# Block-sparse attention and a token/channel mixer in one kernel: keys of two head pairs turned by DMA, and the first pair's keys written from PSUM

## The chip, the cores and the metric

The kernel runs on one core of a Trainium2 chip. The metric is the device time of one execution in microseconds, the median of several runs. A profiled execution gives a trace of every instruction; its span is a little shorter than the time of that execution, which has some work around it. The engines are named as in the profile: PE multiplies matrices (PEld is its weight load), DVE and ACT are the vector and the scalar engine, POOL is GpSimd, SP issues most DMA transfers from one queue, in order.

## The reference

Inputs are `q`, `k`, `v` of shape (4, 8, 768, 64) and the weights of a mixer. Attention picks key blocks of 64 by the mean of their keys, then the mixer works on the result:

```python
k_rep = k.reshape(B, H, n_blocks, block, D).mean(axis=3)
gate_scores = np.einsum('bhsd,bhnd->bhsn', q, k_rep)      # 12 blocks
gate_scores = np.where(causal, gate_scores, -1e9)
# each query keeps its 3 best blocks and its own block, causally
scores = scale * np.matmul(q, k.transpose(0, 1, 3, 2))
attn = softmax(np.where(mask, scores, -1e9))
x = np.matmul(attn, v)                                    # heads side by side: (4, 768, 512)
h = np.maximum(x.transpose(0, 2, 1) @ w_tok1, 0) @ w_tok2 # along the tokens
u = x + h.transpose(0, 2, 1)
out = u + np.maximum(u @ w_ch1, 0) @ w_ch2                # along the channels
```

Which blocks a query keeps depends on close comparisons, so the gate's operands are carried in more than one fp16 number; the scores themselves take fp16.

## The kernel before, in words

**Tiling.** Heads go in 16 pairs, `i` = 0 to 15; four pairs make one batch element `b`. The two heads of a pair fill the 128 partitions (64 dimensions each) when the dimensions lie in partitions, and stand side by side when tokens lie in partitions. A sequence is six tiles of 128 tokens, twelve blocks of 64.

**Preparation of a pair's keys.** `load_qk` (line 350) loads them in fp32 with tokens in partitions (tile `kl`). PE turns them with six fp32 transposes into PSUM: `transposes` (line 406, into a two-bank buffer of the ring `big`, which the scores also use) or, for the pairs below `SPLIT` = 4, `transposes_half` (line 414, three at a time into one bank of the ring `bank`). ACT or DVE then evicts them, times eight, into an fp32 tile `kt` (`evac_t` and `evac_half`, through `scaled` at lines 434 and 436). POOL casts each head's 64 rows to fp16 into the matmul operand `KA` (`cast`, line 490). DVE sums the columns of each block (`ksum`, line 563; for pair 0 straight from PSUM, `ksum_half`, line 428). The sums become the gate's operand: for pairs 0 to 3 in fp32 (`kcopy`, line 516), from pair 4 on as an fp16 number and its fp16 rest (`split_k`, lines 508 and 510).

**Preparation of a pair's queries.** Pairs 0 to 3 go the same way as the keys (`qt`). Pairs 4 to 9 are evicted as an fp16 number and its rest (`evac_q` line 449, `rest_q` line 456). From pair 10 on (`QTURN`) the queries are rounded while tokens are still in partitions: ACT writes the fp16 number (`split_hi`, line 464), DVE the rest (`split_rest`, line 470), and two DMA transposes from SP turn both (`turn_q`, line 475). POOL places each head's rows in the operand `QA`, copying two fp16 numbers as one fp32 (`place_q`, line 496).

**Gate and mask.** PE multiplies queries by block sums (line 525 in fp32, line 541 in fp16 parts), DVE finds the third best (lines 531 to 601), and the resulting mask is turned, by PE (line 611) up to pair 8 and by DMA (line 590) from pair 9 on, and put in twelve further rows of `QA`: the mask rides in the scores' matmul (line 633). ACT takes the exponential (line 647), PE multiplies with the values (line 663), DVE normalises (lines 671 and 682).

**Mixer.** When the four pairs of a batch element are done, PE does the token mix (lines 706 and 718; for `b` = 0 per pair, lines 737 and 751), then the first channel product (line 787) and the second (line 838, in seven products per four blocks; line 894 at the very end).

**What sets the order.** Nothing is ordered by hand. Each step is an `Op` with an engine, a planned duration, its dependencies, the buffers that it takes and a priority. `plan` (line 102) runs through them once, before the kernel is built: on each engine it takes, of what can start soon, the op with the smallest priority, and for steps given with `either` also the engine, ACT or DVE, that ends sooner. The result is a fixed sequence per engine; every engine then works through its own in order. A pair's priorities are ten per pair plus an offset: `PRE[i]` for its preparation, `LAG[b]` for the channel products, `SHIFT` for steps of one kind. Ahead of 17 us of planned time PE's holes are filled with dummy matmuls (line 913). Weights are loaded by POOL (lines 942 to 947); `WAIT` names for each load the cast that it is placed behind, `W0` that of the first, the token weights. SP issues key, query and value loads, turns (`SPO`) and output stores in one sequence; the ring `kt` has three slots, `kl` three, `bank` three, `big` two.

Of the kernel before, what the change touches and what calls it, by code (L numbers as in the profile page):

```python
# [54 lines left out]
HEAD = 15000.0  # L55
INBANK = 16
QTURN = 10
MTURN = 9
TOCC = 1250
QLEAD = 0.0  # L60
# [188 lines left out]
def kernel(  # L249
# [28 lines left out]
    pairs = [(b, h) for b in range(B) for h in range(0, H, 2)]  # L278
    NP = len(pairs)
    RINGS = dict(big=2, bank=3, av=1, ql=3, kl=3, v32=2, kt=3, gs=2, e0=3, e1=3, e2=3, rc=2,  # L280
                 x16=2, h1=1, u=2, uT=1, h2a=1, h2b=1, ob=3, s1=1, s3=1, s4=1, f32=6, qh=2, qr=2, mt=1)

    def const(name, a, dt, eng):
        t = sp.tile(list(a.shape), dt, tag=name, name=name)
# [3 lines left out]
    def sb(tag, shape, dt, name):  # L288
        return sp.tile(shape, dt, tag=tag, bufs=RINGS[tag], name=name)
# [26 lines left out]
    t3_16 = sp.tile([128, HF, 256], F16, tag="t3", name="t3")  # L316
    t4_16 = sp.tile([128, HF, 256], F16, tag="t4", name="t4")
    warm = t1_16[:, 0, :]
    spare = sp.tile([128, 8], F16, tag="spare", name="spare")
    ident32 = sp.tile([128, 128], FP, tag="id32", name="id32")  # L320
    ident16 = sp.tile([128, 128], F16, tag="id16", name="id16")
# [13 lines left out]
    def act(cols, deps, prio, fn, takes=()):  # L335
        return op("ACT", 70 + cols * 0.833, 173 + cols * 0.833, deps, prio, fn, takes)
# [80 lines left out]
    def evac_half(name, src, i, m):  # L417
# [3 lines left out]
            scaled(e, T[name, i][:, S // 2 * m:S // 2 * m + S // 2], T["tr", src, i, m])  # L421
        return f

    def ksum_half(i, m):
        def f():
            if ("kst", i) not in T:
                T["kst", i] = sp.tile([128, NB], FP, tag="kst", bufs=2, name=f"kst_{i}")
            nc.vector.tensor_reduce(out=T["kst", i][:, NB // 2 * m:NB // 2 * m + NB // 2],
                                    in_=T["tr", "kl", i, m].rearrange("p (n w) -> p n w", w=64), axis=AX.X, op=ALU.add)
        return f  # L430
# [21 lines left out]
    def rest_q(i):  # L452
        def f():
            t = sb("qr", [128, S - 128], F16, f"qr_{i}")
            T["qr", i] = t
            nc.vector.scalar_tensor_tensor(out=t, in0=T["tr", "ql", i][:, 128:S], scalar=UP, in1=T["qh", i][:, 128:S],
                                           op0=ALU.mult, op1=ALU.subtract)
        return f

    def split_hi(i):  # L460
# [489 lines left out]
    for i in range(NP):  # L950
# [8 lines left out]
        zq = [op("POOL", 355, 412, [], pre - 1, zero_q(i))] if 0 < i < R else []  # L959
        for t32, src, off in (("kl", k, 0), ("ql", q, 0.1)):  # L960
            bf = Buf(t32)
            if t32 == "ql" and i >= QTURN:
# [16 lines left out]
                O[t32, i] = op("SP", 950, 0, [], pre - 12 + off, load_qk(i, t32, src), [bf], size=1900)  # L979
            name = "kt" if t32 == "kl" else "qt"  # L980
            if i < SPLIT:
                tb = Buf("kt")
                ev, ks = [], []
                for m in range(2):
                    bk = Buf("bank")
                    tr = pe(330, [O["ld", t32, i, m] if i < HALVES else O[t32, i]], pre + off + 0.01 * m, transposes_half(t32, i, m), [bk], tail=320)
                    bf.users.append(tr)
                    first = name == "kt" and i < EARLY
                    if first:
                        ks.append(dve(460, [tr], pre + 0.4, ksum_half(i, m)))  # L990
# [4 lines left out]
                O[name, i], O["half", name, i] = ev[1], ev  # L995
            else:
                big = Buf("big")
                O["tr", t32, i] = pe(660, [O[t32, i]], pre + off, transposes(t32, i), [big], tail=320)
                bf.users.append(O["tr", t32, i])
            if name == "kt":  # L1000
                if i >= SPLIT:
                    tb = Buf("kt")
                    O["kt", i] = either(768, 860, [O["tr", t32, i]], pre + 0.5, evac_t("kt", "kl", i), [tb])
                    big.users.append(O["kt", i])
                for x in range(2):
                    if i < HALVES:
                        for m in range(2):
# [12 lines left out]
                if i < HALVES:  # L1020
                    pass
                elif i < SPLIT:
                    O["kcopy", i] = dve(257, [O["ksum", i]], pre + 1, kcopy(i))
                else:
                    O["kcopy", i] = op("POOL", 1040, 998, [O["ksum", i], O.get(("gate", i - 2))], pre + 1, split_k(i))
            elif i < SPLIT:
                qb = tb
                for x in range(2):
                    if i < HALVES:
                        for m in range(2):  # L1030
                            O["cast", "qt", i, x, m] = op("POOL", 470, 500, ev[m:m + 1] + zq, pre + 4.1 + 0.2 * m, cast(QA, "qt", i, x, S // 2 * m, S // 2 * m + S // 2))
                            qb.users.append(O["cast", "qt", i, x, m])
                        continue
                    O["cast", "qt", i, x] = op("POOL", 865, 822, [O["qt", i]] + zq + last_scores(x), pre + 4.1, cast(QA, "qt", i, x))
                    qb.users.append(O["cast", "qt", i, x])
            else:
                hb, rb = Buf("qh"), Buf("qr")
                O["qh", i] = act(768, [O["tr", t32, i]], pre + 0.6, evac_q(i), [hb])
                O["qr", i] = dve(740, [O["qh", i]], pre + 2, rest_q(i), [rb])
                big.users.append(O["qr", i])  # L1040
                hb.users.append(O["qr", i])
                for x in range(2):
                    O["cast", "qt", i, x] = op("POOL", 457, 503, [O["qh", i]] + zq + last_scores(x), pre + 4.1, place_q(i, x))
                    hb.users.append(O["cast", "qt", i, x])
# [248 lines left out]
    with tc.manual_schedule():  # L1293
# [75 lines left out]
```

## Time and profile before

| | us |
|---|---|
| median of 3 runs | 250.09 (250.06 to 250.19) |
| the profiled execution | 250.11 |
| its span | 248.30 |
| PE busy | 238.0 |
| DVE busy | 185.4 |
| ACT busy | 155.3 |
| POOL busy | 136.2 |
| last transposes of keys (pair 15, line 406) | at 172.3 |
| last wait of the span: final add and store after the last matmul | 245.0 to 248.3 |

The page of the profile gives busy time per engine first. It counts instructions as they overlap: a matmul's record is longer than the time by which it holds up the next one, so what a group of matmuls costs is read from the starts, or from the chain of waits, which tells the pieces in order of time. In rows by engine, a bracket says how long the engine sat idle before the instruction and what ended that.

### The profile page before, as it was taken

The numbers are of one execution on the slowest core, as the hardware profiler recorded it, in microseconds if no ns is written. First come the engines' busy times: TensorE is split into PE (matmuls) and PEld (weight loads), VectorE is DVE, ScalarE is ACT, GpSimd is POOL, SyncE is SP. The second block draws the span as 40 slices with busy tenths as digits, with TensorE's granted clock in tenths as the row PEclk, the third lists the DMA queues.
The fourth block names the chain that finished last, engine by engine and source line by source line (L and its number), as shares of the span: only waits on it lengthen the run. The fifth ranks groups of instructions, "written<-read, shape, count | busy, mean of one in ns | idle before, by whom it ended". The sixth has DMA issues, their size and how long they took to land.

```text
span 248.3 us, 6734 instructions
## 1 busy us (share of the span) xinstructions
PE 238.0 (96%) x2575; PEld 181.8 (73%) x2575; DVE 185.4 (75%) x572; ACT 155.3 (63%) x234; POOL 136.2 (55%) x230
## 2 busy tenths in 40 slices
PE   7898989999999899999999989999999999999994
PEld 5787879767767676888666878677666867766863
DVE  6677768977999799998956999995654769332742
ACT  3576777998688878356656958756687631355210
POOL 8967826465643773589985799706410245500380
PEclk9999999999999999999999999999999999999999
DMA  8999999999992199989999946463210024600033
GB/s 163 204 210 230 194 234 222 192 201 237 181 222 36 29 233 206 189 175 207 240 213 223 205 87 102 105 122 76 87 26 3 1 76 97 195 19 0 3 124 131
DMA packets 105040, 35.38 MB, mean 143 GB/s; under 512 B 98672, under 2 KB 101512, under 8 KB 105008
## 3 DMA queue, kind: packets, MB, share of 16 engines
q1 hardware_dynamic: 100016, 30.45, 62.2%
q0 software_dynamic: 3392, 4.11, 9.9%
q10 hardware_dynamic: 1600, 0.39, 0.8%
q8 instruction: 20, 0.33, 0.6%
q14 instruction: 12, 0.10, 0.1%
HBM read 26.92 MB, written 6.29 MB: 134 GB/s over the span
## 4 chain that ended last, share of the span: by engine, by line
PE 81%; POOL 5%; issue 5%; ACT 3%; DVE 3%; DMA 2%; SPq 1%; POOLq 0%; DVEq 0%; ACTq 0%
PE c L787 23%; PE c L838 18%; PE sps L633 12%; PE aps L663 8%; PE ups L718 3%; PE tok L706 3%; PE tkl L406 3%; PE c L894 2%; PE gps L525 2%; DMA kl<-in_k_dram 2%; ACT e L647 2%; PE tok L737 1%; PE gps L541 1%; PE sps L637 1%; POOL kp L508 1%
## 5 line engine op out<-in xcount | busy, mean ns | idle before, releaser
L647 ACT ACTIVATE e<-sps 128x1024 f16<-128x1024 f32 (+2 forms) x96 | 85.1, 916 | 18.3 <-PE sps L633 15.2
L787 PE MATMUL c<-uT,wc 128*128 128x256 f16 (+1 forms) x384 | 69.3, 326 | 0.0
L633 PE MATMUL sps<-Q,KA 76*128 76x128 f16 (+7 forms) x384 | 52.0, 259 | 1.9 <-ACT e L647 1.1
L860 POOL TENSOR_TENSOR vu<-v,u 128x256 f32<-128x256 f32 x33 | 22.9, 719 | 51.7 <-DVE v L853 51.7
L787 PEld LDWEIGHTS <-wc 128*128 128x128 f16 x384 | 36.2, 98 | 19.6 <-issue 0.2
L490 POOL CAST KA<-kt 64x768 f16<-64x768 f32 (+1 forms) x34 | 27.8, 819 | 30.6 <-ACT kt L434 19.9
L633 PEld LDWEIGHTS <-KA 76*128 76x128 f16 (+1 forms) x384 | 31.3, 98 | 15.2 <-ACT e L647 1.6
L663 PEld LDWEIGHTS <-e 128*128 128x128 f16 x672 | 24.9, 98 | 3.3 <-issue 0.4
L663 PE MATMUL aps<-V,e 128*128 128x65 f16 x672 | 26.6, 193 | 0.4 <-POOL V L383 0.3
L689 ACT ACTIVATE h2a<-c 128x512 f16<-128x512 f32 (+1 forms) x29 | 15.2, 528 | 11.7 <-PE c L787 11.5
L689 ACT ACTIVATE h2b<-c 128x512 f16<-128x512 f32 (+1 forms) x31 | 15.9, 527 | 10.2 <-PE c L787 10.1
L838 PEld LDWEIGHTS <-s 128*128 128x128 f16 x198 | 18.8, 98 | 3.6 <-issue 1.1
L838 PE MATMUL c<-t,s 128*128 128x256 f16 x132 | 17.8, 272 | 1.0 <-DVE ob L874 1.0
L682 DVE TENSOR_TENSOR x<-aps,rc 128x384 f16<-128x384 f32 x32 | 17.6, 550 | 0.5
L653 DVE TENSOR_TENSOR e<-e,m 128x768 f16<-128x768 f16 x24 | 14.6, 608 | 3.6 <-ACT e L647 3.5
L691 DVE TENSOR_SCALAR h2a<-c 128x256 f16<-128x256 f32 (+1 forms) x19 | 9.0, 476 | 10.7 <-PE c L787 10.6
L434 ACT ACTIVATE kt<-tkl 128x768 f32<-128x768 f32 (+1 forms) x16 | 11.7, 729 | 6.6 <-PE tkl L406 3.3
L496 POOL COPY Q<-qh 64x384 f32<-64x384 f32 x24 | 13.8, 576 | 2.2 <-ACT qh L449 1.2
L383 POOL CAST V<-v 128x768 f16<-128x768 f32 x16 | 13.6, 856 | 2.4 <-DMA v<-in_v_dram 1.9
L572 DVE MAX8 m<-gps 128x8 f32<-128x12 f32 x160 | 13.9, 158 | 0.3
L563 DVE TENSOR_REDUCE kst<-kt 128x12 f32<-128x768 f32 x15 | 14.1, 943 | 0.0
L691 DVE TENSOR_SCALAR h2b<-c 128x256 f16<-128x256 f32 (+1 forms) x17 | 8.0, 468 | 8.3 <-PE c L787 8.0
(117 smaller groups left out, 434.1 us busy)
## 6 DMA issues: line engine op xcount, KB each, us to landing
v<-in_v_dram SPq DMA_DIRECT2D x16, 384.0 KB, 5.8
out_dram<-ob SPq DMA_DIRECT2D x23, 256.0 KB, 2.5
kl<-in_k_dram SPq DMA_DIRECT2D x30, 192.0 KB, 5.0
ql<-in_q_dram SPq DMA_DIRECT2D x30, 192.0 KB, 5.1
wc<-in_moe_w_ch_dram POOLq DMA_DIRECT2D x8, 384.0 KB, 6.7
w<-in_moe_w_tok_dram POOLq DMA_DIRECT2D x2, 384.0 KB, 6.5
ql<-in_q_dram ACTq DMA_DIRECT2D x4, 96.0 KB, 3.5
kl<-in_k_dram SPq DMA_DIRECT2D x4, 96.0 KB, 3.1
```

The costliest lines, as they stand in the source:

```text
L490: nc.gpsimd.tensor_copy(out=dst[i % R][x][lo:lo + 64, a:z], in_=T[name, i][lo:lo + 64, a:z])
L563: nc.vector.tensor_reduce(out=kst, in_=T["kt", i].rearrange("p (n w) -> p n w", w=64), axis=AX.X, op=ALU.add)
L633: nc.tensor.matmul(out=p[:, off + a:off + a + n], lhsT=KA[i % R][x][0:rows, 128 * kk:128 * kk + 128], rhs=QA[i % R][x][0:rows, q0 + a:q0 + ...
L647: nc.scalar.activation(out=e[:, 0:width], in_=T["sps", i, x, g][:, 0:width], func=AF.Exp, scale=scale)
L653: nc.vector.tensor_tensor(out=d, in0=d, in1=m0.broadcast_to([128, NJ, 128]), op=ALU.mult)
L663: nc.tensor.matmul(out=p[:, jq, :], lhsT=T["e", i, x, g][:, o:o + 128], rhs=V16[i % (R + 1)][:, x, kk, :], start=(kk == 0), stop=(kk == jq))
L682: nc.vector.tensor_tensor(out=T["x16", b][:, :, 64 * hh:64 * hh + 64], in0=T["aps", i, x][:, :, 0:64], in1=T["rc", i, x].broadcast_to([128 ...
L689: e.activation(out=out, in_=src, func=AF.Relu)
L691: e.tensor_scalar(out=out, in0=src, scalar1=0.0, scalar2=None, op0=ALU.max)
L787: nc.tensor.matmul(out=p, lhsT=wc1_16[:, cc, 128 * fc:128 * fc + 128], rhs=T["uT", b][:, a // 128:e // 128, cc, :], start=(cc == 0), stop= ...
L838: nc.tensor.matmul(out=T["c2" + key, b, j], lhsT=x[:, fc, :], rhs=y[:, fc, :], start=first and fc == 0, stop=fc == HF - 1, skip_group_chec ...
L860: nc.gpsimd.tensor_tensor(out=t, in0=T["v", b, j], in1=T["u", b][:, j + 3 * row, 256 * col:256 * col + 256], op=ALU.add)
```

## The change

It has three parts. **Pairs 14 and 15** (`KTURN`): the keys are rounded with tokens in partitions, the fp16 number by ACT or DVE (`ksplit_hi`) and its rest by DVE (`ksplit_rest`), into one slot of the ring `kt`; a DMA transpose from SP turns the fp16 numbers (`turn_k`) into a new tile `kh` with one slot; POOL places each head's rows as fp32 words (`place_k`). The block sums come from PE: for each of six token tiles and both parts a matmul with the 128x128 part as weight and a constant `two` of two columns (ones in the first 64 rows, ones in the last 64), so that twelve matmuls give twelve block sums in one bank (`ksum_pe`); ACT or DVE copies them out (`ksum_put`). The rounding of a pair's queries is made to wait for that of its keys. **Pair 0**: the fp32 tile `kt` and its four POOL casts go; instead each head's 64 rows of each half go from PSUM to `KA` as fp16, by ACT or DVE (`place_half`), after the block sums of that half. **The order**: `PRE`, `LAG`, `SHIFT` and `W0` have new values; among them pair 0's offset goes from 9.0 to 3.0, and the token weights are placed behind the second query cast of pair 2 in place of the first key cast of pair 3. The preamble fills `two` with three DVE instructions.

```diff
-PRE = [9.0, 1.5, 3.5, 1.5, 4.5, 4.0, 2.5, 3.0, -3.0, -0.5, 8.5, 9.5, 6.0, 8.5, -1.0, -2.5]
-LAG = [5.0, 1.0, -2.0, -2.0]
-SHIFT = {'bias': 0.5, 'sc': -0.7, 'ex': -3.2, 'uadd': 1.0, 'lt': 3.7, 'ch1': -0.8, 'qn2': -0.5, 'av': 1.2, 'tok1': -7.0, 'gate': -0.5, 'qr': 2.3, 'mask': 0.8, 'ksum': 0.5, 'cast': -2.0, 'dg': 2.8, 'half': -0.7, 'top': 3.2, 'put': -1.5, 'kt': -4.0, 'gm': 1.0, 'norm': 1.2, 'kcopy': -6.0, 'tr': 0.5, 'qn': -3.0}
+PRE = [3.0, 1.5, 0.5, 0.5, 3.5, 4.0, 5.0, 5.5, -3.5, -0.5, 9.5, 10.5, 3.0, 6.0, -3.5, -2.0]
+LAG = [5.0, 0.0, 9.0, 6.5]
+SHIFT = {'bias': 0.5, 'sc': -0.7, 'ex': -3.2, 'uadd': 1.0, 'lt': 4.2, 'ch1': -0.8, 'qn2': 2.5, 'av': 2.0, 'tok1': -8.0, 'gate': -0.5, 'qr': 1.2999999999999998, 'mask': -2.0, 'ksum': -0.5, 'cast': -1.5, 'dg': 2.5, 'half': -1.7, 'top': 0.2, 'put': -0.5, 'kt': -4.0, 'gm': -2.7, 'norm': 1.4, 'kcopy': 0.0, 'tr': 0.5, 'v': -1.0, 'relu2': 1.0, 'umix': -0.5, 'relu1': 1.0, 'qh': -4.0}
...
+KTURN = 14
+KHN = 1
...
-W0 = ('kt', 3, 0)
+W0 = ('qt', 2, 1)
...
+    def place_half(i, x, m):
+        def f(e):
+            rows, cols = slice(64 * x, 64 * x + 64), slice(S // 2 * m, S // 2 * m + S // 2)
+            scaled(e, KA[i % R][x][rows, cols], T["tr", "kl", i, m][rows, :])
+        return f
...
+            scaled(e, t[:, 0], T["kl", i])
...
+            nc.vector.scalar_tensor_tensor(out=t[:, 1], in0=T["kl", i], scalar=UP, in1=t[:, 0], op0=ALU.mult, op1=ALU.subtract)
...
+            turn(T["kh", i].rearrange("p (j t) -> p j t", t=128), T["kn", i][:, 0].rearrange("p j d -> p (j d)"))
...
+            nc.gpsimd.tensor_copy(out=KA[i % R][x][lo:lo + 64, :].bitcast(FP), in_=T["kh", i][lo:lo + 64, :].bitcast(FP))
...
+            for j in range(NJ):
+                for c in range(2):
+                    nc.tensor.matmul(out=p[:, 2 * j:2 * j + 2], lhsT=T["kn", i][:, c, j, :], rhs=two, start=(c == 0), stop=(c == 1))
...
+            if t32 == "kl" and i >= KTURN:
+                O[t32, i] = op("SP", 950, 0, [], pre - 12.1 - QLEAD, load_qk(i, t32, src), [bf], size=1900)
+                nb, hb, kb = Buf("kt"), Buf("kh"), Buf("bank")
+                O["kn", i] = either(768, 860, [O[t32, i], O.get(("qn", i - 1))], pre - 4.1, ksplit_hi(i), [nb])
+                O["kn2", i] = dve(940, [O["kn", i]], pre - 4.1, ksplit_rest(i), both=True)
...
+                O["kh", i] = op("SPO", TOCC, 0, [O["kn", i], O.get(("kh", i - 1))], -1.1, turn_k(i), [hb], size=1300)
+                O["ksm", i] = pe(420, [O["kn2", i]], pre + 0.2, ksum_pe(i), [kb])
...
+                O["ksum", i] = either(80, 140, [O["ksm", i]], pre + 0.5, ksum_put(i))
...
+                O["kcopy", i] = op("POOL", 1040, 998, [O["ksum", i], O.get(("gate", i - 2))], pre + 1, split_k(i))
+                for x in range(2):
+                    O["cast", "kt", i, x] = op("POOL", 457, 503, [O["kh", i]] + last_scores(x), pre + 4, place_k(i, x))
...
-                O["qn", i] = act(795, [O[t32, i]], pre - 4, split_hi(i), [nb])
+                O["qn", i] = act(795, [O[t32, i], O.get(("kn", i))], pre - 4, split_hi(i), [nb])
...
-                tb = Buf("kt")
+                tb = Buf("kt") if i >= HALVES or name == "qt" else None
...
+                    if i < HALVES and name == "kt":
+                        for x in range(2):
+                            O["cast", "kt", i, x, m] = either(384, 460, [tr] + ks[m:m + 1], pre + 0.6 + 0.3 * x, place_half(i, x, m))
+                            bk.users.append(O["cast", "kt", i, x, m])
+                        continue
...
-                        for m in range(2):
-                            O["cast", "kt", i, x, m] = op("POOL", 470, 500, ev[m:m + 1], pre + 4 + 0.2 * m, cast(KA, "kt", i, x, S // 2 * m, S // 2 * m + S // 2))
-                            tb.users.append(O["cast", "kt", i, x, m])
+                        continue
...
+        nc.vector.memset(two, 0.0)
+        for n in range(2):
+            nc.vector.memset(two[64 * n:64 * n + 64, n:n + 1], 1.0)
```

More of the change, by code (lines that the diff above doesn't have):

```diff
@@ L280 @@
     RINGS = dict(big=2, bank=3, av=1, ql=3, kl=3, v32=2, kt=3, gs=2, e0=3, e1=3, e2=3, rc=2,
-                 x16=2, h1=1, u=2, uT=1, h2a=1, h2b=1, ob=3, s1=1, s3=1, s4=1, f32=6, qh=2, qr=2, mt=1)
+                 x16=2, h1=1, u=2, uT=1, h2a=1, h2b=1, ob=3, s1=1, s3=1, s4=1, f32=6, qh=2, qr=2, mt=1, kh=KHN)
     def const(name, a, dt, eng):
@@ L318 @@
     warm = t1_16[:, 0, :]
+    two = sp.tile([128, 2], F16, tag="two", name="two")
     spare = sp.tile([128, 8], F16, tag="spare", name="spare")
@@ L457, in f, with ksplit_hi, ksplit_rest, turn_k @@
                                            op0=ALU.mult, op1=ALU.subtract)
+        return f
+    def ksplit_hi(i):
+        def f(e):
+            t = sb("kt", [128, S], FP, f"kn_{i}").bitcast(F16).rearrange("p (c j d) -> p c j d", c=2, d=2 * D)
+            T["kn", i] = t
+            scaled(e, t[:, 0], T["kl", i])
+        return f
+    def ksplit_rest(i):
+        def f():
+            t = T["kn", i]
+            nc.vector.scalar_tensor_tensor(out=t[:, 1], in0=T["kl", i], scalar=UP, in1=t[:, 0], op0=ALU.mult, op1=ALU.subtract)
+        return f
+    def turn_k(i):
+        def f():
+            T["kh", i] = sb("kh", [128, S], F16, f"kh_{i}")
+            turn(T["kh", i].rearrange("p (j t) -> p j t", t=128), T["kn", i][:, 0].rearrange("p j d -> p (j d)"))
+        return f
+    def place_k(i, x):
+        def f():
+            lo = 64 * x
+            nc.gpsimd.tensor_copy(out=KA[i % R][x][lo:lo + 64, :].bitcast(FP), in_=T["kh", i][lo:lo + 64, :].bitcast(FP))
+        return f
+    def ksum_pe(i):
+        def f():
+            p = ps("bank", [128, NB], "kps")
+            T["kps", i] = p
+            for j in range(NJ):
+                for c in range(2):
+                    nc.tensor.matmul(out=p[:, 2 * j:2 * j + 2], lhsT=T["kn", i][:, c, j, :], rhs=two, start=(c == 0), stop=(c == 1))
+        return f
+    def ksum_put(i):
+        def f(e):
+            kst = sp.tile([128, NB], FP, tag="kst", bufs=2, name=f"kst_{i}")
+            T["kst", i] = kst
+            copy(e, kst, T["kps", i])
         return f
@@ L961 @@
             bf = Buf(t32)
+            if t32 == "kl" and i >= KTURN:
[3 more added lines that the diff above has]
+                O["kn2", i] = dve(940, [O["kn", i]], pre - 4.1, ksplit_rest(i), both=True)
+                bf.users += [O["kn", i], O["kn2", i]]
+                O["kh", i] = op("SPO", TOCC, 0, [O["kn", i], O.get(("kh", i - 1))], -1.1, turn_k(i), [hb], size=1300)
+                O["ksm", i] = pe(420, [O["kn2", i]], pre + 0.2, ksum_pe(i), [kb])
+                nb.users += [O["kh", i], O["ksm", i]]
+                O["ksum", i] = either(80, 140, [O["ksm", i]], pre + 0.5, ksum_put(i))
+                kb.users.append(O["ksum", i])
+                O["kcopy", i] = op("POOL", 1040, 998, [O["ksum", i], O.get(("gate", i - 2))], pre + 1, split_k(i))
+                for x in range(2):
+                    O["cast", "kt", i, x] = op("POOL", 457, 503, [O["kh", i]] + last_scores(x), pre + 4, place_k(i, x))
+                    hb.users.append(O["cast", "kt", i, x])
+                continue
             if t32 == "ql" and i >= QTURN:
@@ L992 @@
                             O["kcopy", i, m] = dve(257, ks[m:], pre + 0.45, kcopy(i, NB // 2 * m, NB // 2 * m + NB // 2))
+                    if i < HALVES and name == "kt":
[3 more added lines that the diff above has]
+                        continue
                     ev.append(either(384, 460, [tr] + ks[m:m + 1] + (ev if i >= HALVES else []), pre + 0.5 + off, evac_half(name, t32, i, m), [tb] if m == 0 else []))
                     bk.users += ks[m:m + 1] + ev[m:m + 1]
-                O[name, i], O["half", name, i] = ev[1], ev
+                if ev:
+                    O[name, i], O["half", name, i] = ev[1], ev
             else:
@@ L1006 @@
                     if i < HALVES:
-                        for m in range(2):
-                            O["cast", "kt", i, x, m] = op("POOL", 470, 500, ev[m:m + 1], pre + 4 + 0.2 * m, cast(KA, "kt", i, x, S // 2 * m, S // 2 * m + S // 2))
-                            tb.users.append(O["cast", "kt", i, x, m])
+                        continue
                     else:
```

## The prediction

> **What bounds the kernel now.** I read the first page for the engines' shares, then busy time by stretches of 10 us, then the list of what the matmul engine (PE) waited for, and last the chain of waits with the timelines of the stretches that the change touches.
>
> ```profile
> span 248.3 us, 6734 instructions
> PE 238.0 (96%) x2575; PEld 181.8 (73%) x2575; DVE 185.4 (75%) x572; ACT 155.3 (63%) x234; POOL 136.2 (55%) x230
> ```
>
> PE is busy 238.0 of 248.3 us, so 10.3 us are idle. The average hides where. The stretches (columns: stretch, its length, then busy us and count for PE, PEld, DVE, ACT, POOL, then granted clock and DMA) show it:
>
> ```profile
> 10.00:20.00 10.00, 9.06 (x108) 7.94 (x108) 7.40 (x33) 7.96 (x13) 7.55 (x12) 1.00 1.21 214
> 140.00:150.00 10.00, 9.01 (x116) 7.70 (x115) 9.85 (x19) 6.49 (x9) 9.38 (x16) 1.00 0.67 140
> 170.00:180.00 10.00, 10.00 (x113) 7.02 (x110) 6.04 (x24) 6.17 (x11) 6.23 (x13) 1.00 0.23 70
> 240.00:248.30 8.30, 5.03 (x36) 3.23 (x33) 2.10 (x5) 0.00 (x0) 1.82 (x3) 1.00 0.34 127
> ```
>
> From 150 to 230 us PE is never idle, and the granted clock is 1.00. There a microsecond of PE work is a microsecond of the end. The last 3.3 us (8.30 less 5.03) are the final add and store, which the change leaves alone. All else that can be won lies before 60 us and in two single waits later. The list of PE's waits names them (total, times, longest):
>
> ```profile
> PE c L838 <- DVE ob L874: 1.0, 1, 1.0
> PE gps L541 <- POOL kp L510: 0.8, 1, 0.8
> PE sps L633 <- ACT Q L695: 0.6, 1, 0.6
> PE tok L737 <- DVE x L682: 0.5, 1, 0.5
> ```
>
> With these go two waits for exps (0.80 at 32.06, 0.30 at 27.81), one of 0.27 for values at 53.85 and one of 0.21 for block sums at 20.78: 4.5 us in all behind 15 us of the span. Ahead of that, PE fills its holes with dummy matmuls, 6.5 us of them, which are no work.
>
> **Part 1: keys of pairs 14 and 15.** Removed per pair: six fp32 transposes on PE, their eviction and the sum over 768 columns. Added: a rounding and a rest in token layout, one DMA turn, twelve fp16 matmuls of two columns, a small copy, two placings. What PE pays for the transposes is read from the chain; what a short fp16 matmul with a new 128x128 weight costs, from the gate matmuls of 48 columns, whose busy times overlap, so the starts count:
>
> ```profile
> 172.47 0.66 PE tkl L406 x6
> ```
>
> ```profile
> 151.98 0.19 PE L541 MATMUL gps<-kp,qh 128*128 128x48 f16 x1
> 152.01 0.18 PE L541 MATMUL gps<-kp,qr 128*128 128x48 f16 x1
> ...
> 152.21 0.18 PE L541 MATMUL gps<-kp,qr 128*128 128x48 f16 x1
> 152.24 0.83 PE L663 MATMUL aps<-V,e 128*128 128x65 f16 x21
> ```
>
> Ten of them take 152.24 - 151.98 = 0.26 us, 26 ns each. Two columns aren't in the trace. Above, they are bounded by the fp32 gate matmuls (line 525, ten in 1.11 us, 0.11 each: 1.33 us per pair, a loss of 0.67); below, they can't be free, since each loads a weight of its own, and I put the floor at half the 48-column row, 0.16 us. I take 26 ns, the row with the same type and the same weight load: 12 x 0.026 = 0.31 us. **PE saves 2 x (0.66 - 0.31) = 0.70 us**, between a gain of 1.0 and a loss of 1.3. Pair 15's transposes stand at 172 us and pair 14's at 130.7 us, both on the chain, with no PE hole within 5 us: the gain counts in full if nothing new is waited for.
>
> [...]
>
> Other engines, per pair. ACT: rounding from SBUF 0.84 (line 464, 842 ns) for the eviction's 0.81, plus the small copy, some 0.2. DVE: the rest of 768 columns at the 640-column row (line 470, median 817 ns, up to 1151) is 0.98, at most 1.38, for the sum's 0.94. POOL: two placings at 0.58 (line 496) for two casts at 0.86 (line 490), 0.57 less. All of these lie beside PE: from 150 to 190 us the busiest of them, DVE, stays under 9.6 of 10, and in 170-180 it has 4 us free. I count them at nothing; if cover is gone at 140-150, where DVE is busy 9.85, the +0.04 to +0.44 of DVE comes through for pair 14.
>
> SP and DMA: two more turns, each some 1.2 us of SP's queue (line 475, median 1254 and 1227 ns) and 2.6 to 4.9 us to landing. SP takes its queue in order; behind a turn that waits for its rounding stand the loads of later pairs, the query and mask turns and output stores. Pair 14's keys are issued at 120.7, pair 15's at 128.2; pair 15's first scores start at 177.6. That is tens of microseconds for a delay of some six, so nothing is counted; without it a wait of PE of the size of its longest now, 0.99, is the price. The freed two-bank buffer can only let scores start earlier, worth nothing where PE has no hole.
>
> **Part 2: pair 0's keys straight from PSUM.** Four POOL casts go (507 ns each, 2.0 us). Two evictions of 128 rows (ACT, 492 ns) become four of 64 rows, for ACT or DVE. As a row's columns set the time, I take 0.49 each: 0.98 more for ACT and DVE. The chain of the head (start, us, what) has no POOL piece:
>
> ```profile
> 7.14 0.57 DVE kst L428
> 7.73 0.49 ACT kt L434
> 8.22 0.39 ACT qt L434
> 8.65 0.85 PE gps L525 x6
> 9.50 0.13 PE bps L611 x2
> ```
>
> So POOL's relief shortens nothing there, and the two extra evictions can stand ahead of the query eviction that the gate waits for. DVE is free between 7.70 and 7.80 and can take one of a couple, so of 0.98 I count **+0.2 us**, about what is left when both engines share the halves (0.49 beside 0.32 of block-sum copies). Bounds: +0.98 if all stands in the chain; -0.9 if pair 0's new priority (its offset falls from 9.0 to 3.0) closes the hole before pair 1's gate (0.66 dummies and 0.25 idle at 13.7 to 14.6). The three small fills of the new constant, some 0.11 us each like the other short ones, fall in DVE's 0.44 idle before 5.01.
>
> **Part 3: the new order.** Offsets, shifts and the point of the first weight load change the order on every engine. One step can be priced. The token weights are issued behind a cast of pair 3's keys; now behind the second cast of pair 2's queries:
>
> ```profile
> 21.09 1.71 POOL L490 CAST Q<-qt 64x768 f16<-64x768 f32 x2
> 26.02 0.87 POOL L942 DMA_DIRECT2D w<-in_moe_w_tok_dram  x1
> 34.51 1.50 PE L737 MATMUL tok<-x,w 128*128 128x128 f16 x24
> ```
>
> In the old places that is 22.8 instead of 26.0, 3.2 us earlier. Landing took 5.8 us, to about 31.8; now about 28.6. So the first token matmuls, 0.67 us for a pair's twelve, can fill the wait of 0.80 at 32.06. **I count -0.4 us**, half of that wait: bounds 0 and -0.8. The load moves into a stretch where the DMA engines are busy throughout, and can delay key loads. Everything else of the order I set at 0, with 0.8 to both sides, about one of the single waits listed.
>
> **Sum.** The profiled run took 250.11 us: span 248.30 and 1.81 around it (0.02 over the median of the runs). 250.11 - 0.70 + 0.2 - 0.4 = **249.2 us**, 0.4% less.
>
> **Rivals.**
> A. The new order also closes the holes: the 0.80 and 0.61 waits and the 0.78 of the gate at 82.9 shrink by half beyond the sum, about 1.0 more: 248.2. For: there are 4.5 us of such holes. Against: each has another cause. 12%.
> B. Early holes eat the gain: the 0.98 of the head comes in full and the token weights fill nothing: 250.11 - 0.70 + 0.98 = 250.4; or half of it, 250.0. 13%.
> C. The change doesn't give PE what it says: the two-column matmuls are paced by their issue and not by weights and columns. From 55 ns each (0.66 / 12, half of the fp32 gate's 0.11) PE saves nothing: 250.11 + 0.2 - 0.4 = 249.9. Against: the 48-column row. 5%. [...]
> D. **Slower: ACT and DVE pace the scores up to 35 us, and get more to do.** The 0.98 delays pair 0's mask, its exps start later, and the mask copy of pair 1, for which PE already waits 0.61 at 19.83, stands behind them again: 0.98 + 0.61 = 1.59, 250.11 - 0.70 + 1.59 = 251.0. It decides from about 1.2 us of added PE idle before 35 us (0.70 saved and 0.5 to be seen). For: the chain of the head runs over ACT and DVE. Against: ACT is idle 2.0 of 10 us there. 22%.
>
> **Chances.** My forecast 48%. A measurement here can tell about 0.2%, 0.5 us, from no change. Faster: forecast and A, 60%. Same: B and C, 18%. Slower: D, 22%. The range reaches from A's 248.2 to D's 251.0, widened by 0.1 at the bottom: 248.1 to 251.0; with half of A and of D beyond its ends 17% are left out.
>
> **What would show it.** Part 1: 60 key transposes of line 406 for 72, and twelve matmuls in about 0.31 us by their starts; 0.66 or more says C. PE still without holes from 150 to 230, else a turn or a rest came late. Part 2: the second gate of pair 0 starts within 0.3 of 8.65; later than 9.3 says D. Part 3: token weights issued near 22.8, and no 0.8 wait at 32. I am wrong if PE's idle time plus dummies, not its work, makes the difference.

## The result and the profile after

The changed kernel takes 251.97 us (251.27 to 254.08), the one before 250.29 in the same comparison; the ratio is 1.0068 [1.0042, 1.0094]. I had forecast 249.2 and "faster": it is slower, and the time lies above my range. About a third of the executions of the kernel before show a mean granted clock of 0.993 in place of 1.00 and take some 1.36 us longer, so the single times below are medians of executions at 1.00 (before: 250.09, 61 of 91; after: 251.66), while each ratio is that of its whole comparison, with its 95% interval.

The first two lines of the page of after:

```profile
span 249.5 us, 6756 instructions
PE 238.4 (96%) x2585; PEld 181.5 (73%) x2585; DVE 189.0 (76%) x575; ACT 155.9 (62%) x238; POOL 133.5 (54%) x226
```

PE's busy time says little here (238.0 before, 238.4 after): it holds the dummies and the overlap of records. So I split PE's time by the starts of its matmuls. Each form has a usual distance to the next start (216 ns for 512 columns of fp16, 109 for 256 of fp16 and for 128 of fp32, 25 for 48 and for 2); the count times that is **work**, and what a start is late beyond it, dummies included, is **loss**. Before: work 228.26, loss 15.53. After: 227.55 and 17.59. Work falls by 0.71, loss grows by 2.06, and the last matmul starts 1.35 later (244.75, 246.10).

Loss by stretch, before and after, in us:

| stretch | before | after |
|---|---|---|
| 0 to 30 | 9.37 | 9.63 |
| 30 to 40 | 0.98 | 0.47 |
| 40 to 50 | 1.04 | 1.77 |
| 50 to 110 | 2.50 | 2.01 |
| 110 to 120 | 0.09 | 1.56 |
| 120 to 150 | 1.20 | 1.43 |
| 150 to the end | 0.34 | 0.72 |

Up to 110 us the two kernels are level: the sums are 13.90 and 13.88. Then one stretch of 10 us gives away 1.47. The view of busy time by stretches shows the same (columns as before: stretch, length, busy us of PE, PEld, DVE, ACT, POOL, clock, DMA):

```profile
30.00:40.00 10.00, 9.78 (x173) 8.81 (x171) 7.37 (x27) 6.80 (x10) 3.16 (x5) 1.00 1.05 210
40.00:50.00 10.00, 9.23 (x145) 8.04 (x142) 8.25 (x28) 8.25 (x11) 5.78 (x15) 1.00 0.95 196
110.00:120.00 10.00, 8.80 (x101) 6.66 (x99) 8.63 (x15) 7.00 (x10) 7.60 (x14) 1.00 0.93 217
```

In these stretches PE was busy 9.21, 9.41 and 10.00 before. Now it is idle 1.20 us of 110 to 120, where it had no hole at all, and no engine looks full there: DVE has 1.4 us free, POOL 2.4. The list of PE's waits names who was late:

```profile
PE c L837 <- DVE ob L922: 0.6, 1, 0.6
PE c L837 <- DVE ob L924: 0.6, 1, 0.6
```

Both are the channel product waiting for DVE to add a finished block and so free its PSUM. The timeline of that moment (start, us, engine, line, operation; the bracket is the idle time before and who ended it) says why DVE was late:

```profile
112.46 0.72 POOL L933 TENSOR_TENSOR ob<-vu,pc 128x256 f32<-128x256 f32 x1
112.77 2.97 DVE L520 SCALAR_TENSOR_TENSOR qn<-ql,qn 128x640 f16<-128x640 f32 x1
113.14 1.92 POOL L910 TENSOR_TENSOR vu<-v,u 128x256 f32<-128x256 f32 x3
115.67 0.18 DVE L721 RECIPROCAL rc<-aps 128x6 f32<-128x6 f32 x1
...
116.60 0.40 DVE L922 TENSOR_TENSOR ob<-u,c 128x256 f32<-128x256 f16 x1
...
117.06 1.02 PE L837 MATMUL c<-uT,wc 128*128 128x512 f16 x4 [0.63 <-DVE ob L922]
...
118.20 0.40 DVE L924 TENSOR_TENSOR ob<-vu,c 128x256 f32<-128x256 f32 x1
```

DVE's rest of pair 12's queries (line 520) takes 2.97 us; the median of the six on this line is 0.83. It starts while POOL is in the first of four instructions that follow each other without a gap (line 933, three of line 910, 112.46 to 115.06) and ends 0.68 after the last of them, a little less than the shortest on this line takes (0.79). By these times it did next to nothing until POOL was through. "Busy" counts that as DVE's work, which is why the stretch shows DVE at 8.63 with fewer instructions, 15 for 29 in the same stretch before. Behind it in DVE's fixed sequence stand the two additions that PE needs.

The trace of before has the same thing at another place, where it is the 0.99 that my prediction listed as PE's largest single wait for DVE:

```profile
144.02 1.17 POOL L596 COPY Q<-mt 12x320 f32<-12x320 f32 x2
...
144.80 2.69 DVE L819 TENSOR_TENSOR s<-h2a,h2b 128x768 f16<-128x768 f16 x1
145.15 1.91 POOL L860 TENSOR_TENSOR vu<-v,u 128x256 f32<-128x256 f32 x3
...
147.41 0.41 DVE L874 TENSOR_TENSOR ob<-vu,c 128x256 f32<-128x256 f32 x1
...
147.87 0.82 PE L838 MATMUL c<-t,s 128*128 128x256 f16 x6 [0.99 <-DVE ob L874]
```

DVE's instruction starts in POOL's second mask copy (line 596), and POOL's three sums follow that without a gap. I had read only the last of these lines, as a wait, and not the 2.69 that made it; the shortest of the eleven on that line takes 0.54, the median 0.74.

### The profile page after: what moved, and what is told of

Same layout as the page of the kernel before. It is cut to its first block, busy times and chain, and to the rows that moved or that the text cites. A ratio compares the mean times of both kernels' runs of the same rounds, so it can differ in the third digit from the quotient of the medians.

```text
span 249.5 us, 6756 instructions
## 1 busy us (share of the span) xinstructions
PE 238.4 (96%) x2585; PEld 181.5 (73%) x2585; DVE 189.0 (76%) x575; ACT 155.9 (62%) x238; POOL 133.5 (54%) x226
## 4 chain that ended last, share of the span: by engine, by line
PE 72%; DVE 9%; issue 6%; POOL 6%; ACT 3%; DMA 2%; DVEq 0%; POOLq 0%; ACTq 0%
PE c L837 22%; PE c L888 13%; PE sps L683 11%; PE aps L713 7%; PE ups L768 3%; PE tok L756 3%; PE tkl L409 2%; PE c L944 2%; ACT e L697 2%; POOL vu L910 2%; DMA qr<-qn 2%; PE gps L575 2%; PE tok L787 1%; DVE qn L520 1%; PE gps L591 1%
## 5 line engine op out<-in xcount | busy, mean ns | idle before, releaser
L697 ACT ACTIVATE e<-sps 128x768 f16<-128x768 f32 (+2 forms) x96 | 83.8, 916 | 15.6 <-PE sps L683 12.1
L683 PE MATMUL sps<-Q,KA 76*128 76x128 f16 (+7 forms) x384 | 51.3, 259 | 2.5 <-ACT e L697 1.7
L910 POOL TENSOR_TENSOR vu<-v,u 128x256 f32<-128x256 f32 x33 | 24.2, 757 | 46.5 <-DVE v L903 46.3
L540 POOL CAST KA<-kt 64x768 f16<-64x768 f32 x26 | 21.4, 824 | 36.7 <-ACT kt L443 33.9
L739 ACT ACTIVATE h2a<-c 128x512 f16<-128x512 f32 (+1 forms) x29 | 14.6, 514 | 12.1 <-PE c L837 11.9
L703 DVE TENSOR_TENSOR e<-e,m 128x768 f16<-128x768 f16 x24 | 15.3, 638 | 1.9 <-ACT e L697 1.9
L741 DVE TENSOR_SCALAR h2a<-c 128x256 f16<-128x256 f32 (+1 forms) x19 | 9.6, 507 | 8.3 <-PE c L837 8.0
L888 PEld LDWEIGHTS <-h2b 128*128 128x128 f16 x132 | 12.6, 97 | 2.3 <-issue 0.5
L546 POOL COPY Q<-qh 64x384 f32<-64x384 f32 x24 | 13.1, 544 | 2.2 <-ACT qh L458 1.2
L888 PEld LDWEIGHTS <-h2a 128*128 128x128 f16 x132 | 12.8, 98 | 1.9
```

The lines of the kernel that those rows point to most:

```text
L540: nc.gpsimd.tensor_copy(out=dst[i % R][x][lo:lo + 64, a:z], in_=T[name, i][lo:lo + 64, a:z])
L683: nc.tensor.matmul(out=p[:, off + a:off + a + n], lhsT=KA[i % R][x][0:rows, 128 * kk:128 * kk + 128], rhs=QA[i % R][x][0:rows, q0 + a:q0 + ...
L697: nc.scalar.activation(out=e[:, 0:width], in_=T["sps", i, x, g][:, 0:width], func=AF.Exp, scale=scale)
L703: nc.vector.tensor_tensor(out=d, in0=d, in1=m0.broadcast_to([128, NJ, 128]), op=ALU.mult)
L739: e.activation(out=out, in_=src, func=AF.Relu)
L741: e.tensor_scalar(out=out, in0=src, scalar1=0.0, scalar2=None, op0=ALU.max)
```

## The experiments

Two theories. **T1: the parts do what I worked out, and the new order loses the time**, by that meeting of DVE and POOL at 113 us above all. **T2: the parts bring the loss**: the keys' rounding holds slots of the ring `kt` or fills ACT and DVE, the other loads stand behind the new turns, or the head is longer. All kernels here compute the reference in full.

| kernel | ratio to before | us at clock 1.00 (executions there) |
|---|---|---|
| after | 1.0068 [1.0042, 1.0094] | 251.66 (9 of 12) |
| order alone | 1.0289 [1.0249, 1.0329] | 257.0 (2 of 6) |
| both parts, old order | 0.9991 [0.9968, 1.0014] | 249.68 (4 of 12) |
| part 1, old order | 0.9972 [0.9952, 0.9992] | 249.40 (9 of 12) |
| part 2, old order | 1.0056 [1.0040, 1.0073] | 250.56 (1 of 7) |
| both parts, old order, new `W0` | 1.0130 [1.0098, 1.0161] | 252.65 (3 of 6) |
| after without part 1 | 1.0123 [1.0075, 1.0171] | 252.77 (3 of 4) |
| after, three POOL sums on DVE | 1.0019 [0.9989, 1.0049] | 250.66 (10 of 12) |
| after, DVE's rest moved | 1.0012 [0.9995, 1.0029] | 250.30 (10 of 12) |
| after, four `kt` slots | 1.0044 [1.0021, 1.0067] | 251.58 (11 of 12) |
| the last two together | 0.9994 [0.9974, 1.0014] | 250.63 (12 of 12) |
| both parts, old order, dummies at 20 us | 0.9965 [0.9945, 0.9985] | 249.65 (11 of 12) |
| part 1, old order, dummies at 20 us | 0.9958 [0.9937, 0.9979] | 249.42 (10 of 11) |
| keys of pairs 12 to 15, old order | 1.0180 [1.0147, 1.0213] | 254.09 (2 of 6) |
| keys of pairs 10 to 15, old order | 1.0144 [1.0111, 1.0178] | 253.41 (2 of 5) |

**The order and the parts, one by one.** From before, the new constants alone; and from after, the old constants back:

```diff
...
-LAG = [5.0, 1.0, -2.0, -2.0]
...
+LAG = [5.0, 0.0, 9.0, 6.5]
...
-W0 = ('kt', 3, 0)
+W0 = ('qt', 2, 1)
```

> The kernel before with the four new order constants alone. Theory 1 (the new order loses it: a wait of VectorE for GpSimd and one of ScalarE for a DMA stand in front of the matmul engine, while the parts themselves save 0.7 us): 251.0 to 252.5 us, slower than before by about 1 to 2 us. Theory 2 (rival D of the prediction: the parts load ScalarE and VectorE and lose it in the first 35 us): within 0.5 us of before or faster, 249.6 to 250.6.

> The changed kernel with the four order constants of before: parts 1 and 2 alone, planned anew. Theory 1: 249.2 to 250.2 us, the 0.7 us of matmul work saved, less some tenths of new waits. Theory 2: 251 us or more, with over 1 us of added idle time and dummies of the matmul engine before 35 us.

Measured: +7 us for the order alone, 249.68 for the parts in the old order. So the parts aren't what costs: T2 falls as the main cause. But the order alone is far worse than the order with the parts, and outside both ranges expected, so its price is no fixed term that could be added: the constants go with one list of steps, and each step taken in or out makes `plan` place all engines anew. In the trace of the order alone PE's longest waits are 2.4 for an ACT copy, 1.5 and 1.4 for DVE, none of them in after.

**Each part in the old order.** `KTURN = 16` takes part 1 out; giving pair 0 its fp32 tile and casts back takes part 2 out; the third kernel has both and only `W0` new.

```diff
-KTURN = 14
+KTURN = 16
```

```diff
-                tb = Buf("kt") if i >= HALVES or name == "qt" else None
+                tb = Buf("kt")
...
-                    if i < HALVES and name == "kt":
...
```

> The kernel before with part 1 alone (keys of pairs 14 and 15), its four order constants kept, planned anew. Theory 1 (the parts are sound, the order of the changed kernel loses the time): 249.3 to 249.9 us in executions at a granted clock of 1.00, and 0.71 us less matmul work. Rival: the added turns, rounding and rest take the 0.7 back in waits after 110 us: 250.1 us or more.

> The kernel before with part 2 alone (pair 0's keys straight from PSUM), its four order constants kept, planned anew. Theory 1: 0.2 us slower by the head (two more evictions on ScalarE and VectorE), 250.2 to 250.5 us. Rival D of the prediction: 1.0 to 1.6 us slower, 251 us or more. A third case, that GpSimd's relief helps: 249.5 us.

> Parts 1 and 2 with the order constants of before, and the point of the first weight load alone as in the changed kernel. The prediction's term of -0.4 us (half of the wait of 0.8 us at 32 us filled): 0.2 to 0.6 us faster than parts 1 and 2 without it, 249.0 to 249.5 us at a granted clock of 1.00. Rival: the token matmuls only move, what is won at 32 us is given back by 50 us as in the changed kernel (0.51 won, 0.73 lost): no gain.

Measured: part 1 gives 249.40, 0.69 below before. Part 2 gives 250.56 in one execution, +0.47, and +0.28 where it is added to part 1. Part 2 alone has 0.45 more loss than before, 0.21 of it by 30 us and 0.29 in 40 to 50. The new `W0` costs 3.0, where a gain was expected and no gain was the rival. Its loss is spread over the span (against both parts without it: 1.3 us more by 30 us, 1.2 in 50 to 60, 2.0 in 110 to 150, 1.1 in 150 to 160), with no wait over 0.7 but the dummies' own. The 1.3 by 30 us are the lower clock of the execution that was profiled; in 30 to 50, where the load was to help, it loses 0.3 less. One constant moves one load, and the sequences of PE, DVE, ACT and POOL come out different from 24 us (POOL) or 32 us (the others) up to some 170.

**The meeting of DVE and POOL, taken away from both sides.** First the three POOL sums of line 910 go to DVE; then POOL is left alone, and DVE's rest is put behind the next four instructions of DVE's sequence:

```diff
-            nc.gpsimd.tensor_tensor(out=t, in0=T["v", b, j], in1=T["u", b][:, j + 3 * row, 256 * col:256 * col + 256], op=ALU.add)
+            (nc.vector if (b, j) == (0, 2) else nc.gpsimd).tensor_tensor(out=t, in0=T["v", b, j], in1=T["u", b][:, j + 3 * row, 256 * col:256 * col + 256], op=ALU.add)
```

```diff
+    late = O["qn2", 12]
+    behind = [o for o in order[order.index(late) + 1:] if o.eng == "DVE"][3]
+    order.remove(late)
+    order.insert(order.index(behind) + 1, late)
...
```

> The changed kernel in its own order, with the three sums that follow the queries' rest at 112.8 us on VectorE in place of GpSimd. Theory 1 (VectorE's rest of pair 12's queries took 2.97 in place of 0.8 us as GpSimd kept going beside it): the rest takes under 1.3 us, and the matmul engine's two waits in 110 to 120 us, 1.21 in all, fall under 0.5: 0.5 to 1.3 us faster than the changed kernel, though VectorE gets some 1.2 us of sums. Rival (the rest is slow for a reason of its own, or VectorE has too much to do there): it stays above 2.5 us, and the waits grow by the sums' time, to 2 us or more.

> The changed kernel in its own order but for one VectorE instruction: the rest of pair 12's queries, which took 2.97 us beside GpSimd's four, goes behind the next four of VectorE's (reciprocal, block sums, an output sum, a normalisation). Theory 1: the output sum that the matmul engine waits for at 117.1 is done some 2 us sooner, the two waits of 1.21 us in 110 to 120 fall under 0.5, and the time falls by 0.6 to 1.4 us from 251.97. Rival: VectorE has too much to do there whatever the order; the waits keep over 1 us.

The timeline with the three sums on DVE, and then with the rest moved (the execution profiled took 253.91; its clock was half from 23.6 to 27.0 us, and 1.00 here):

```profile
112.74 1.09 DVE L520 SCALAR_TENSOR_TENSOR qn<-ql,qn 128x640 f16<-128x640 f32 x1
```

```profile
117.44 0.82 DVE L520 SCALAR_TENSOR_TENSOR qn<-ql,qn 128x640 f16<-128x640 f32 x1
117.45 1.34 POOL L560 TENSOR_TENSOR kp<-kst,kp 64x12 f16<-64x12 f32 x2
```

In the first, one POOL instruction is left in front: it ends 0.41 after DVE's starts, and DVE's ends 0.68 after that. In the second DVE starts just ahead of POOL, takes its 0.82, and now POOL's pair takes 1.34 where it takes 0.69 in after. The kernel with the fourth slot added to this (below; 250.38 in its profiled execution) has the same two rows with 0.81 and 1.33. The time falls by 1.00 and by 1.36 from after's 251.66. Loss in 110 to 120 goes from 1.56 to 0.56 with the three sums moved, and with the rest moved PE is busy 9.86 of these 10 us. Only one instruction is at another place in the second kernel, so this meeting is shown to be the greater part of what the change lost: 1.36 of the 1.57 between before and after.

**The other candidates.** At 148.25 the rounding of pair 15's keys on ACT waits 2.04 us for a DMA turn that still reads a `kt` slot, the exps stand behind it, and PE waits 1.10. A fourth slot, in the same order of steps, takes that away; one kernel has both this and the moved rest. And part 1 taken out of after shows whether it makes the meeting.

```diff
+    RINGS["kt"] = 4
```

> The changed kernel in its own order, with four buffers in place of three behind the key and query tiles. Theory 1: ScalarE's rounding of pair 15's keys no longer waits 2.0 us for the DMA turn that frees its buffer at 148.2, and the matmul engine's wait of 1.10 us for the exps at 150.1 falls under 0.3: 0.8 to 1.2 us faster than the changed kernel, 250.6 to 251.2 us by its median of 251.97. Rival: the rounding is followed by three exps that are late anyway; the wait of 1.1 stays and the time too.

> The changed kernel in its own order with both waits taken away: the rest of pair 12's queries four places later, and four buffers behind the key and query tiles. If ScalarE's wait at 148 us costs the matmul engine its 1.1 us: 249.1 to 249.6 us at a granted clock of 1.00 (with the first wait alone gone: 250.3). If it is given back later, as it was without the first: 250.1 to 250.5.

> The changed kernel with its new order constants and part 2, without part 1, planned anew. If the new constants fit only the one kernel that they stand in: 2 us or more off the changed kernel in its sum of waits, 253 to 258 us. Rival, that the new order is bad by itself and part 1 takes nothing: the changed kernel's 251.7 and 0.7 us of matmul work, 252.4 us.

Of the kernel with four slots and the old place of the rest:

```profile
140.00:150.00 10.00, 10.00 (x134) 8.60 (x133) 9.48 (x20) 8.09 (x12) 7.64 (x13) 1.00 1.06 196
150.00:160.00 10.00, 9.63 (x134) 7.93 (x133) 9.39 (x45) 8.07 (x11) 9.32 (x17) 1.00 0.18 62
```

PE's hole of 0.99 in 140 to 150 is gone, and 150 to 170 has new ones: the loss in 140 to 170 is 1.30 for 1.30. The kernel isn't measurably faster (251.58 for 251.66), and together with the moved rest it gives 250.63, not less than the 250.30 of the rest alone. So this wait was real and its removal worth nothing: behind it PE now waits for other work, POOL's mask copies (0.5 in two) by name. Without part 1 the meeting is there all the same (line 520 takes 2.98), and the time is 252.77: part 1 doesn't make it.

**More of part 1.** If one pair saves 0.35, four or six pairs should save more; `KTURN` is 12, then 10, in the old order.

> Part 1 alone with the order constants of before, for the pairs 12 to 15 in place of 14 and 15, planned anew. If part 1's gain is matmul work that nothing takes back, two pairs more save another 0.71 us: 248.5 to 248.9 us at a granted clock of 1.00 (part 1 for two pairs: 249.4). Rival: the added turns and rests of pairs 12 and 13 meet VectorE and SyncE where they are full (110 to 140 us): 249.4 us or more.

> As the kernel with pairs 12 to 15, for the pairs 10 to 15. If nothing takes it back: 1.42 us less than with two pairs, 247.8 to 248.2 us at a granted clock of 1.00. Rival: 249.4 us or more, with new waits of the matmul engine between 90 and 140 us for VectorE or for turns.

Measured: PE's work falls as it should, to 226.85 and 226.14, but the loss is 20.94 and 20.86, and the times are 254.09 and 253.41. By their work they should take 248.7 and 248.0, so 5.4 us are lost, in places from 70 to 170 us. Whether the plan loses them, or the added turns and rests meet DVE and SP where those are full, as the rival had it, these two runs don't separate: an order tuned for these steps wasn't tried.

**The clock.** With part 2 in the old order 14 of 19 executions had the lower clock, before 30 of 91. Seven dummy matmuls of 256 columns go into PE's hole of 0.77 at 20 us:

```diff
+                        if (i, x, g, kk) == (1, 0, 0, 0):
+                            for _ in range(7):
+                                nc.tensor.matmul(out=p[:, 512:768], lhsT=warm[:, 0:128], rhs=warm, start=True, stop=True, skip_group_check=True)
```

> Parts 1 and 2 with the order constants of before, and seven dummy matmuls more in the hole of 0.77 us in front of pair 1's scores at 20 us (they write columns that the scores overwrite). Theory: 8 of 12 executions of that kernel had a granted clock of 0.993 and took 1.3 us longer, as the clock is halved for 3.4 us when the matmul engine has done little between 19 and 22 us; with the hole filled that share falls to 3 of 12 or less, and the median from 250.9 to 249.5 to 249.9 us; executions at 1.00 stay at 249.4 to 249.9. Rival: the lower clock has nothing to do with that hole; its share stays at half or more, the median at 250.9.

> Part 1 alone with the order constants of before, and the seven dummy matmuls in the hole at 20 us. Executions at a granted clock of 1.00 as without the dummies, 249.2 to 249.6 us; executions at 0.993, 3 of 12 without the dummies, 1 of 12 or none; median 249.3 to 249.5. Rival: the share of the lower clock stays at 3 of 12, the median at 249.43.

Measured: 1 of 12 and 1 of 11 executions at the lower clock, where it was 8 of 12 and 3 of 12 without the dummies; only the first fall is clear. At a clock of 1.00 they change nothing (249.65 for 249.68, 249.42 for 249.40): what they win is that the lower clock is rarer. By their ratios both kernels are 0.3 to 0.4% faster than before; part 1 alone with the dummies, 0.9958 [0.9937, 0.9979], is the best of the study, within the others' intervals. The kernel before with these dummies wasn't tried.

## Why the prediction was wrong

**What bounds the kernel: right as far as it went.** PE's starts set the end: work less 0.71 and loss plus 2.06 make the 1.35 by which the last matmul is later. That what can be won lies before 60 us and in two single waits wasn't refuted; I didn't ask what could be lost behind it. PE without a hole says that the other engines come in time in this order, not that they have time to spare.

**Part 1: right, and to the size.** 60 transposes of line 409 for 72, and the twelve short matmuls, by the timeline of after:

```profile
145.75 0.44 PE L500 MATMUL kps<-two,kn 128*128 128x2 f16 x12
146.05 0.81 PE L888 MATMUL c<-t,s 128*128 128x256 f16 x6
```

From 145.75 to 146.05 is 0.30, 25 ns each; 0.31 was taken. Forecast -0.70, PE's work -0.71, the time of part 1 alone -0.69. That the last comes so close is in part luck: in its trace the loss of 140 to 150 is 1.06 less than before (the wait at 147.87 is gone), and 130 to 140 and 150 to 160 lose 0.63 and 0.51 more. The rival of a slow issue (C), 55 ns each, is out. What I counted at nothing for SP, DMA and ACT came to about nothing in part 1 by itself, but only in the sum. The sign that PE has no hole from 150 to 230 us fails by little: 0.11 in 150 to 160 and 0.08 in 200 to 210.

**Part 2: right in size in the head.** The second gate of pair 0 in after:

```profile
9.02 0.82 PE L575 MATMUL gps<-ks,qt 128*128 128x24 f32 x6 [0.31 <-DVE ks L566]
```

With part 2 alone it starts at 8.86; 8.65 was before, and I had given 0.3 of room: +0.37 and +0.21. The 0.49 that I took for an eviction of 64 rows held on ACT in after (0.48 for 64x384, 0.49 for 128x384); on DVE it took 0.56 (0.55 for 128x384). Loss by 30 us is 0.26 higher; +0.2 was forecast. The 0.29 that part 2 alone loses in 40 to 50, where the transposes of a pair's keys start 0.27 late, I had not looked for. Rival D's mechanism, 1.6 us in the head, isn't there, though its sign came true. Of rival A, holes did shrink (none of the 0.80 at 32.06, 0.5 of the 0.8 at 82.9 left), but others opened. (Rival B's smaller value adds up to 249.9, not 250.0; nothing hangs on it.)

**Part 3, the token weights: the wait went, the gain didn't stay.** Their load in after:

```profile
22.95 0.87 POOL L992 DMA_DIRECT2D w<-in_moe_w_tok_dram  x1
```

22.8 was forecast. The weights landed 7.5 us later, not 5.8, and the first token matmuls start at 31.4 for 34.5. The 0.80 at 32.06 is gone, and 30 to 40 loses 0.51 less, where I counted 0.4. But 40 to 50 loses 0.73 more, most of it in three late starts: 0.29 of token matmuls at 42.14, 0.20 of PE's transposes of keys at 45.82, 0.17 of the product with the values at 46.82. The transposes are as late with part 2 alone, so not all of this is the weights'. By these stretches the term was +0.22 and not -0.4: I asked what hides the wait, and not what is late next.

**The step that failed: "Everything else of the order I set at 0, with 0.8 to both sides, about one of the single waits listed."** Measured: what is left of the loss, 2.06 - 0.26 - 0.22 = +1.58, of which 1.47 lies in 110 to 120: the meeting of DVE and POOL, which gives back 1.36 us when it alone is taken away. With it the sum is -0.71 + 0.26 + 0.22 + 1.58 = 1.35. A zero in the middle was no reading of the profile. An order that is planned anew is a draw for each engine's sequence, and the draws here, old constants with new steps or new with old, gave +3, +5.4 (which may hold a price of the added steps) and +7 us, and with both parts in the old order +0.5 of loss. The rule I had written down, "I am wrong if PE's idle time plus dummies, not its work, makes the difference", is what happened. The kind of loss could have been suspected, if not its place: the trace of before has a DVE instruction of 2.69 us for 0.74, with POOL's run beside it and PE's wait of 0.99 behind it, and the change moves both engines' sequences.

**What stays open.** The moved rest leaves 250.30, some 0.6 above both parts in the old order. The largest late wait of its trace is 1.9 for exps in 140 to 160, the place that the fourth slot clears without a gain, so that doesn't explain the 0.6. That trace is of an execution of 253.91, and DVE and POOL meet in it once more: at 172.16 a DVE instruction (line 703) takes 3.06 beside five of POOL's (the 24 of this line take 17.3 in all, 15.3 in after), and 170 to 180 loses 1.12 for 0.11 in after. Whether the executions at 250.3 have that too is in no trace. At a clock of 1.00 the executions of after spread from 251.27 to 253.20, those of before from 249.74 to 250.68; one execution of each was profiled, so what differs between them stays open. Why part 2 makes the lower clock more frequent is not settled either.

## What to carry to other kernels

Price a change of order apart from the change of work: put the new steps into the old order first, and look at both. Ahead of that, look in the trace for instructions that take a multiple of their own usual duration, and at what ran beside them; behind PE's waits of 0.63 and 0.99 here stood the long instruction before the releaser, of 2.97 and 2.69. A wait that is removed counts only when the next stretch has been read, since the same time can be given back 10 us later.

## What the hardware showed

**DVE and POOL held each other up, and twice DVE's instruction lasted through a whole run of POOL's.** A DVE instruction with two tensors in SBUF took 2.97 beside four POOL instructions in a row (0.83 in the median), 2.69 beside a mask copy and three more (0.74), 1.09 beside one; when DVE was just ahead, POOL's pair took 1.34 for 0.69. In each of these the engine that began first took no longer (POOL's three sums 1.92 and 1.91, its single instruction 0.72, DVE 0.82), and the other was late. At 112.77 in after and at 144.80 in before, DVE's instruction began while POOL was in the first of its back-to-back instructions or in the copy ahead of them, and ended 0.68 and 0.43 after the last of the sums. It isn't always so. In after, 3 us earlier:

```profile
109.02 2.75 POOL L910 TENSOR_TENSOR vu<-v,u 128x256 f32<-128x256 f32 x3
109.38 0.91 DVE L873 TENSOR_TENSOR h2a<-s,h2a 128x768 f16<-128x768 f16 x1
```

Here DVE got in behind POOL's first sum (0.91 for 0.54 at the shortest), and POOL's three took 2.75 where they take 1.92 at 113. What decides between the two is in no trace, nor by what the one engine holds up the other.

**The granted clock was half for 3.4 us, soon after two microseconds in which PE was busy 0.59 of the time.** The profiled execution of part 1 in the old order had the lower clock; its microseconds one by one:

```profile
19.00:20.00 1.00, 0.39 (x7) 0.27 (x6) 0.66 (x2) 0.95 (x3) 1.00 (x2) 1.00 1.00 219
20.00:21.00 1.00, 0.79 (x13) 0.64 (x10) 0.97 (x4) 0.69 (x2) 0.94 (x2) 1.00 0.98 216
...
22.00:23.00 1.00, 1.00 (x23) 0.73 (x21) 0.90 (x9) 0.00 (x0) 0.83 (x1) 0.73 1.22 243
23.00:24.00 1.00, 1.00 (x5) 0.55 (x4) 1.00 (x8) 0.33 (x1) 0.00 (x0) 0.50 1.10 212
...
25.00:26.00 1.00, 1.00 (x11) 0.94 (x10) 0.86 (x2) 0.51 (x1) 0.30 (x1) 0.57 1.18 218
```

The granted clock is half from about 22.5 to 25.9, 3.4 us, though PE was busy 0.79 of the microsecond from 20 and 0.39 of the one before; the rest of the span is at 1.00. Two more executions with the lower clock, profiled, show the same. With the new `W0` PE was busy 0.39 and 0.79 in 19 to 21, and the clock was half from about 22.8 to 26.2; with DVE's rest moved it was 0.39 and 0.76 in 20 to 22, and half from about 23.6 to 27.0. But both parts in the old order, with 0.52 and 0.74 in 19 to 21, kept 1.00 in the profiled execution. And without part 1 the mean clock of 20 to 30 was 0.66, half for an estimated 6.8 us (0.34 of 10 us, doubled). What decides whether the lower clock follows is in no trace. Seven dummies in the hole, some 0.76 us of work that nobody needs, took it from 8 of 12 executions to 1 of 12, in the kernel with both parts.
